# A fused attention and MoE kernel: a fourth unit of work with v in float32, a third buffer for q and M, and one ordering edge on ScalarE

## The chip, the core and the metric

The kernel runs on one core of a Trainium2 chip. The metric is device time in microseconds (us), the median of three runs; smaller is better. The engines are TensorE (PE in the profile, with PEld for its weight loads), VectorE (DVE), ScalarE (ACT), GpSimd (POOL) and SyncE (SP), which here only issues DMAs. Each engine works through its own list of instructions in order, and semaphores tie the lists together.

## What is computed

Two steps follow each other. The first is attention with a memory, for 4 batches, 8 heads, 576 tokens and 64 columns a head. The second is a feed-forward block on its result, 2304 tokens of 512 columns, with a hidden width of 2048:

```python
scores = (q @ k.T) / sqrt(D), causal;  a = softmax(scores);  local = a @ v
q_p = phi(q)                           # max(q, 0) + min(exp(q), 1)
mem_out = (q_p @ M_prev) / (q_p @ z_prev + 1e-6)
x = g * mem_out + (1 - g) * local      # g = sigmoid(beta), one number a head
h = x @ w_in;  r = max(h, 0);  out = (r * r) @ w_out
```

## The kernel before

**Units.** Attention is cut into units: a batch b, a pair p of heads, and a list of query tiles. The list `order` starts with batch 0, tiles [1, 2], pairs 0 to 3 (units one to four, `order[0]` to `order[3]`) and goes on with batch 0, tiles [3, 4], pairs 0 to 3 (units five to eight). The first 64 tokens of each batch are handled ahead of all units by `first_tokens`. `attention` (line 354) handles one unit. It takes exp and phi of q (lines 388 to 402), the memory part `pm` (line 445), and then for each query tile the scores `sp` (line 479), the masked copy `e` with its row bound (line 500), the exponential (line 520), the weights transposed, the product with v into `acc` (lines 572 to 590), and the sum into `memx` (line 600).

**Two ways to v.** The flag `full` is true for the first `NEF` units with tiles [1, 2]. With it the weights `e` stay float32: PE transposes them into `pxa` (line 535), ScalarE copies these to `aF` (line 540), and PE multiplies `aF` by v in float32 (line 579). Without it v and the weights are split into a high and a low float16 part (lines 410 to 433, 558 and 560), a DMA on SP's queue transposes the weights (line 564), PE multiplies float16 parts (lines 585 to 590), and VectorE adds up the two parts (line 592). The first `NES` = 6 units take their scores from float32 q and k as they are; later ones split them first (lines 369 to 379).

**Loads.** `loads` (line 341) issues the DMAs of a unit: `kd` (k, one buffer), `qm` (M and q, `QB` buffers) and `vv` (v, `VVB` = 2 buffers). A unit calls it for the next unit before its own scores. A load waits until the buffer that it takes has been read for the last time.

**Feed-forward blocks.** Tokens go through `moe` (line 723) in blocks of 256: eight rounds j of an up product (lines 747 to 749, 24 matmuls), Relu and square on ScalarE (lines 753 and 754), a high and a low part (`gh`, `gl`), and a down product (lines 737 to 739, 12 matmuls), which stands one round behind. Block 0 is the first 64 tokens of all batches. In its round j = 6 it also prepares block 1: `prefetch` (line 625) reads three quarters of block 1's tokens back from the DRAM tensor `xd`, into which units one to three were written (line 611), transposes them into `px` (line 635), transposes the last quarter straight from unit four's `memx` (line 637, `tail`), and makes `xh` and `xl` (lines 640 and 641). `px` and `up` share two PSUM buffers (tag "up"), so the up product of block 0's last round needs a `px` that has been read.

**What sets the order.** Each engine's list is set when the kernel is built, by a scheduler that plays the program against a model of the chip. A change of a few instructions moves many others. `later` (line 148) adds an edge that only orders: the instruction x stands on its engine behind the one kept in `gate`. `ORD` (line 82) builds units two to four together with block 0, and the rest of the units behind them.

Of the kernel before, what the change touches and what calls it, by code (L numbers as in the profile page):

```python
# [8 lines left out]
F32 = mybir.dt.float32  # L9
# [6 lines left out]
ALU = mybir.AluOpType  # L16
# [22 lines left out]
GHN = 4  # L39
GLV = range(7)  # L40
VMIN = 2.0**-80
NEF = 3
NES = 6
PXT = 'av'
PXE = 'aa'
PHI = 1
QB = 2
VVB = 2
ZW = D + 1
MW = 576  # L50
# [42 lines left out]
def fused_kernel(ctx: ExitStack, tc: tile.TileContext, t0_d, kk_d, qv_d, beta, w_in, w_out, out):  # L93
    nc = tc.nc
# [17 lines left out]
        out=mask, in_=mask, pattern=[[-1, MW]], compare_op=ALU.is_ge, fill=-1e30, base=448, channel_multiplier=1  # L112
# [33 lines left out]
    gate = {}  # L146

    def later(eng, x):
        if eng in gate:
            tc.add_manual_dep(x.ins, gate[eng].ins.name, AFTER, reason="first tokens lead")  # L150
        return x
# [189 lines left out]
    def loads(b, p, tiles):  # L341
        qa, qb = QT[tiles[0]][0], sum(QT[tiles[-1]])
        kd = at.tile([P, S], F32, tag="kd", name="kd", bufs=KB)
        nc.sync.dma_start(kd[:, :qb], kk_d[b, p, :, :qb])
        qm = at.tile([P, 2 * ZW + SQ], F32, tag="qm", name="qm", bufs=QB)
        qa, qb = qa - D + 2 * ZW, qb - D + 2 * ZW
# [7 lines left out]
    def attention(b, p, tiles, ld, after, early, sfull, full):  # L354
# [13 lines left out]
        if not sfull:  # L368
# [4 lines left out]
                out=ql[:, qa:qb], in0=q_raw[:, qa:qb], in1=qh[:, qa:qb].bitcast(F32), op=ALU.subtract  # L373
# [11 lines left out]
        pe = at.tile([P, 2, S], F32, tag="e", name="pe", bufs=EB)[:, 0]  # L385
        w = slice(qa, qb)
        lead = (b, p, tiles) == order[0]
        ex = nc.scalar.activation(pe[:, w], q_raw[:, w], AF.Exp)
        if lead:
            later("s2", ex)  # L390
        ph = pe if sfull else q_raw
        if PHI and not sfull:
            nc.scalar.activation(q_raw[:, w], q_raw[:, w], AF.Relu)
            nc.vector.scalar_tensor_tensor(
                out=q_raw[:, w], in0=pe[:, w], scalar=1.0, in1=q_raw[:, w], op0=ALU.min, op1=ALU.add
            )
        else:
# [3 lines left out]
                out=ph[:, w], in0=q_raw[:, w], scalar=0.0, in1=pe[:, w], op0=ALU.max, op1=ALU.add  # L401
# [3 lines left out]
        if not full:  # L405
# [11 lines left out]
                out=vy, in0=vy, scalar1=VMIN, scalar2=2.0**-VEXP, op0=ALU.max, op1=ALU.mult  # L417
# [6 lines left out]
            if VL[late] == "d":  # L424
                nc.scalar.activation(vh, vr, AF.Copy, scale=vy)
                for h in range(2):
                    nc.vector.scalar_tensor_tensor(
                        out=vl[:, h], in0=vr[:, h], scalar=vy, in1=vh[:, h], op0=ALU.mult, op1=ALU.subtract
# [8 lines left out]
        for grp in (tiles[:2], tiles[2:]):  # L437
# [4 lines left out]
            for j, i in enumerate(grp):  # L442
# [8 lines left out]
                out=nm[:, :ng], in0=pv[:, :, :, D], scalar=1e-6,  # L451
                in1=gi[:, None, h0 : h0 + 2].to_broadcast([P, ng, 2]), op0=ALU.add, op1=ALU.mult,
# [4 lines left out]
                out=memx[:, i0 - 1 : i0 - 1 + ng].rearrange("p i (h d) -> p i h d", h=2),  # L457
                in0=pv[:, :, :, :D],
                in1=nm[:, :ng, :, None].to_broadcast([P, ng, 2, D]),
                op=ALU.mult,  # L460
# [50 lines left out]
        for i in [t for t in TORD if t in tiles]:  # L511
# [6 lines left out]
            for h in range(2):  # L518
                bs = mx[:n, h, ns - 1 : ns]
                ex = nc.scalar.activation(  # L520
                    e[:n, h, :ke], e[:n, h, :ke], AF.Exp, bias=bs, scale=-1.0, accum_out=sm[:n, h : h + 1]
                )
            behind[:] = [ex]
            u0, ur = e[:n, :, 0:D], e[:n, :, D:ke]
            if full:
# [3 lines left out]
                for b0 in range(0, 2 * nb, 4):  # L529
                    bn = min(4, 2 * nb - b0)  # L530
                    px = ps.tile([P, 4, P], F32, tag=PXT, name="pxa", bufs=2)
                    for x in range(bn):
                        h, c = divmod(b0 + x, nb)
# [9 lines left out]
            else:  # L543
# [15 lines left out]
                for x, o0, w in ((ur, P, i * P), (u0, 0, D)):  # L559
                    nc.vector.scalar_tensor_tensor(  # L560
                        out=av[:, :, o0 + w : o0 + 2 * w], in0=x, scalar=SC, in1=av[:, :, o0 : o0 + w],
# [4 lines left out]
                out=sm[:n], in0=sm[:n], scalar=1e-9, in1=gm[:n, h0 : h0 + 2] if full else vz[:n],  # L566
# [6 lines left out]
            if full:  # L573
                s3 = acc[:, :, 0]
# [7 lines left out]
            else:  # L582
# [8 lines left out]
                s3 = at.tile([P, 2, D], F32, tag="s3", name="s3", bufs=1)  # L591
# [6 lines left out]
            for h in range(2 if FX[late] != "p" or full else 0):  # L598
                xo = memx[:n, i - 1, h * D : (h + 1) * D]
                nc.vector.scalar_tensor_tensor(  # L600
                    out=xo, in0=s3[:n, h], scalar=sm[:n, h : h + 1], in1=xo,
# [23 lines left out]
    def prefetch(b, blk, tail=None):  # L625
        nk = NK if tail is None else NK - 1
        xh = mo.tile([P, NK, BLK], F32R, tag="xh", name="xh", bufs=2)
        xl = mo.tile([P, NK, BLK], F32R, tag="xl", name="xl", bufs=2)
        for t in range(2):
            r0 = QT[1 + 2 * blk + t][0]  # L630
            src = mo.tile([P, DM], F32R, tag="x", name="xn", bufs=XB)
            nc.sync.dma_start(src.bitcast(F32)[:, : nk * P], xd[b][r0 : r0 + P, : nk * P])
            px = ps.tile([P, NK, P], F32R, tag="up", name="px", bufs=2)
            for k in range(nk):
                nc.tensor.transpose(px[:, k], src[:, k * P : (k + 1) * P], identr)
            if tail is not None:
                nc.tensor.transpose(px.bitcast(F32)[:, nk], tail[:, t], ident)
            px = px.bitcast(F32)
            ts = slice(t * P, (t + 1) * P)
            nc.scalar.copy(xh[:, :, ts], px)  # L640
            nc.vector.tensor_tensor(out=xl[:, :, ts], in0=px, in1=xh[:, :, ts].bitcast(F32), op=ALU.subtract)
        return xh, xl

    def pair_tiles():
# [78 lines left out]
    def moe(n):  # L723
# [17 lines left out]
        for j in range(NF // 2):  # L741
# [20 lines left out]
            if n == NBLK - 3 and j in (3, PJ):  # L762
                if j == 3:
                    xq.append(pair_tiles())
                pair_prefetch(xq[-1], int(j == PJ))
                yield
            elif j == PJ and n + 1 < NBLK:
                assert n > 0 or last
                xq.append(prefetch(*blocks[n + 1], *last))
                last.clear()  # L770
                yield
# [48 lines left out]
    order = []  # L820
# [8 lines left out]
    def attn(i0, i1):  # L829
        for i in range(i0, i1):  # L830
            ld = nxt.pop()

            def after():
                if i + 1 < len(order):
                    nxt.append(loads(*order[i + 1]))

            yield from attention(*order[i], ld, after, i < NEARLY, i < NES, i < NEF and max(order[i][2]) < 4)

# [60 lines left out]
```

## Time and profile before

| what | value |
|---|---|
| time, median of 3 runs | 578.53 us (578.21 to 580.98) |
| the profiled execution | 578.71 us, span from first to last instruction 576.9 us |
| PE busy | 550.8 us (95% of the span) |
| DVE, ACT, POOL busy | 414.0, 349.6, 63.7 us |
| granted TensorE clock, mean | 0.994 of full speed |

In the page's strip of 40 slices PE stands at nine tenths or more from 10% of the span on, with one weaker slice (8 at a quarter of the way, near 100 us), where the granted clock falls to 7 tenths. Matmuls are pipelined, so the time that a matmul costs is read from one start to the next, not from its own duration. In the profile's rows an instruction on float32 operands at lines 479, 445 and 579 shows as two rows. The rows themselves stand further down, in numbered groups.

### The profile page before, as it was taken

How to read it: one execution, taken by the hardware profiler on the slowest of the kernel's cores; microseconds unless marked ns; L12 is line 12 of the kernel's file. 1: busy time of each engine (PE TensorE's matmuls, PEld its weight loads, DVE VectorE, ACT ScalarE, POOL GpSimd, SP SyncE). 2: the span in 40 equal slices, each digit the busy share in tenths (PEclk: the TensorE clock that was granted, in tenths of full speed). 3: DMA queues.
4: the chain of work that ended last, by engine and by line, in shares of the span. 5: the costliest groups of instructions: out<-in, count | busy, mean ns of one | idle time of the engine just before them, and what ended most of it. 6: DMA issues, size and time to landing. Idle time of an engine off the chain costs nothing.

```text
span 576.9 us, 11597 instructions
## 1 busy us (share of the span) xinstructions
PE 550.8 (95%) x4259; PEld 478.6 (83%) x4259; DVE 414.0 (72%) x1323; ACT 349.6 (61%) x792; POOL 63.7 (11%) x45
## 2 busy tenths in 40 slices
PE   5489998898999999999999999999999999999997
PEld 5378886787888888898988988889889898888885
DVE  6989989897989888989695988969787523212121
ACT  4589976767868767877567675665756222212213
POOL 3749560012010000000000000000000000000000
PEclk9999999799999999999999999999999999999999
DMA  8857654875665466676456736675244610000001
GB/s 310 341 192 286 228 168 111 174 162 136 138 150 159 109 183 151 149 185 168 110 108 124 149 78 163 115 189 143 56 84 83 128 37 1 36 2 0 1 0 73
DMA packets 124856, 74.71 MB, mean 129 GB/s; under 512 B 97152, under 2 KB 110464, under 8 KB 124800
## 3 DMA queue, kind: packets, MB, share of 16 engines
q1 hardware_dynamic: 124800, 73.98, 49.7%
q8 instruction: 33, 0.54, 0.4%
q14 instruction: 23, 0.19, 0.1%
HBM read 41.59 MB, written 8.78 MB: 87 GB/s over the span
## 4 chain that ended last, share of the span: by engine, by line
PE 63%; DVE 12%; ACT 10%; DMA 9%; issue 3%; POOL 1%; SPq 1%; ACTq 0%; DVEq 0%; POOLq 0%
PE oacc L677 8%; PE up L747 6%; PE up L749 6%; PE up L748 6%; PE oacc L737 6%; PE oacc L739 6%; PE oacc L738 6%; PE sp L479 5%; DMA vv<-in_qv_dram 4%; ACT e L520 3%; PE up L692 3%; PE up L691 3%; PE up L693 3%; PE acc L590 2%; PE pm L445 2%
## 5 line engine op out<-in xcount | busy, mean ns | idle before, releaser
L747 PE MATMUL up<-xh,w 128*128 128x256 f32 x448 | 129.5, 289 | 0.0
L748 PE MATMUL up<-xl,w 128*128 128x256 f32 x448 | 128.9, 288 | 0.0
L749 PE MATMUL up<-xh,w 128*128 128x256 f32 x448 | 128.4, 287 | 0.0
L520 ACT ACTIVATE e<-e,mx 128x320 f32<-128x320 f32 (+3 forms) x128 | 77.6, 608 | 50.1 <-DVE memx L600 34.1
L737 PE MATMUL oacc<-w,gh 128*128 128x512 f32 x224 | 89.9, 402 | 0.0
L747 PEld LDWEIGHTS up<-xh,w 128*128 128x128 f32 x448 | 86.0, 192 | 2.9 <-issue 0.6
L738 PE MATMUL oacc<-w,gh 128*128 128x512 f32 x224 | 88.4, 395 | 0.0
L748 PEld LDWEIGHTS up<-xl,w 128*128 128x128 f32 x448 | 86.1, 192 | 2.2
L739 PE MATMUL oacc<-w,gl 128*128 128x512 f32 x224 | 86.4, 397 | 0.4 <-DVE gl L759 0.4
L749 PEld LDWEIGHTS up<-xh,w 128*128 128x128 f32 x448 | 86.1, 192 | 0.7
L560 DVE SCALAR_TENSOR_TENSOR a<-e,a 128x128 f16<-128x128 f32 x116 | 64.1, 566 | 31.1 <-ACT a L558 30.1
L558 ACT ACTIVATE a<-e 128x128 f16<-128x128 f32 x116 | 55.0, 524 | 10.9 <-DMA aT<-a 9.9
L753 ACT ACTIVATE r<-up 128x512 f32<-128x512 f32 x56 | 32.7, 584 | 43.2 <-PE up L749 29.0
L702 DVE CAST gh<-r 128x512 fp32r<-128x512 f32 x15 | 6.4, 427 | 62.4 <-ACT r L701 62.4
L739 PEld LDWEIGHTS oacc<-w,gl 128*128 128x128 f32 x224 | 41.5, 188 | 9.0 <-DVE gl L759 0.9
L738 PEld LDWEIGHTS oacc<-w,gh 128*128 128x128 f32 x224 | 42.3, 189 | 6.6
L500 DVE CUSTOM_DVE_ANT_0 e<-sp,mask 128x320 f32<-128x320 f32 (+3 forms) x128 | 47.0, 417 | 0.9 <-PE sp L479 0.7
L737 PEld LDWEIGHTS oacc<-w,gh 128*128 128x128 f32 x224 | 42.3, 189 | 6.4
L700 ACT ACTIVATE r<-up 128x512 f32<-128x512 f32 x16 | 9.6, 597 | 60.8 <-PE up L693 60.8
L759 DVE TENSOR_TENSOR gl<-r,gh 128x512 fp32r<-128x512 f32 x56 | 38.9, 695 | 2.6 <-ACT gh L756 1.8
L677 PE MATMUL oacc<-w,gh 128*128 128x512 f32 x120 | 36.8, 389 | 0.0
L590 PE MATMUL acc<-vs,aT 128*128 128x128 f16 x302 | 36.7, 220 | 0.0
(153 smaller groups left out, 1160.2 us busy)
## 6 DMA issues: line engine op xcount, KB each, us to landing
raw<-in_w_in_dram SPq DMA_DIRECT2D x11, 512.0 KB, 7.2
vv<-in_qv_dram SPq DMA_DIRECT2D x16, 320.0 KB, 3.3
raw<-in_w_out_dram SPq DMA_DIRECT2D x9, 512.0 KB, 6.6
kd<-in_kk_dram SPq DMA_DIRECT2D x16, 288.0 KB, 3.1
out_dram<-o SPq DMA_DIRECT2D x16, 256.0 KB, 2.1
xd<-memx SPq DMA_DIRECT2D x31, 128.0 KB, 1.9
xn<-xd SPq DMA_DIRECT2D x14, 256.0 KB, 2.9
qm<-in_qv_dram SPq DMA_DIRECT2D x8, 321.0 KB, 2.9
```

Of the source, the lines that this page charges most:

```text
L500: nc.vector.tensor_tensor_reduce(out=e[:, h, ka:kb], in0=sps[:, h, cs], in1=mask[:, 448 - q0 + ka : 448 - q0 + kb], scale=-0.125, scalar=3 ...
L520: ex = nc.scalar.activation(e[:n, h, :ke], e[:n, h, :ke], AF.Exp, bias=bs, scale=-1.0, accum_out=sm[:n, h : h + 1])
L558: nc.scalar.mul(av[:, :, o0 : o0 + w], x, SC)
L560: nc.vector.scalar_tensor_tensor(out=av[:, :, o0 + w : o0 + 2 * w], in0=x, scalar=SC, in1=av[:, :, o0 : o0 + w], op0=ALU.mult, op1=ALU.sub ...
L590: nc.tensor.matmul(o2, aT[:, h * nb + c, :n], vs[:, h, c], start=False, stop=c == i)
L677: mms.append(nc.tensor.matmul(acc[t], g[:, ts], w_out_op(f, part), start=s0, stop=s1))
L737: nc.tensor.matmul(acc[t], gh[:, u, ts], w_out_op(f, 0), start=f == 0, stop=False)
L738: nc.tensor.matmul(acc[t], gh[:, u, ts], w_out_op(f, 1), start=False, stop=False)
L739: nc.tensor.matmul(acc[t], gl[:, u, ts], w_out_op(f, 0), start=False, stop=f == NF - 1)
L747: nc.tensor.matmul(up[:, u, :], w_in_op(f, k, 0), xh[:, k, :], start=k == 0, stop=False)
L748: nc.tensor.matmul(up[:, u, :], w_in_op(f, k, 0), xl[:, k, :], start=False, stop=False)
L749: nc.tensor.matmul(up[:, u, :], w_in_op(f, k, 1), xh[:, k, :], start=False, stop=k == NK - 1)
```

## The change

Three things change. `NEF` goes from 3 to 4, so unit four (batch 0, pair 3, tiles [1, 2]) takes the float32 way to v. `QB` goes from 2 to 3, so `qm` has three buffers. And the exponential of q of the sixth unit (`order[5]`) gets an ordering edge on ScalarE: it stands behind the last copy to `xh` of block 1's `prefetch` (the key "v3" is set and not used).

```diff
-NEF = 3
+NEF = 4
...
-QB = 2
+QB = 3
...
         lead = (b, p, tiles) == order[0]
+        second = (b, p, tiles) == order[5]
         ex = nc.scalar.activation(pe[:, w], q_raw[:, w], AF.Exp)
         if lead:
             later("s2", ex)
+        if second:
+            later("s3", ex)
...
-            nc.scalar.copy(xh[:, :, ts], px)
-            nc.vector.tensor_tensor(out=xl[:, :, ts], in0=px, in1=xh[:, :, ts].bitcast(F32), op=ALU.subtract)
+            c = nc.scalar.copy(xh[:, :, ts], px)
+            d = nc.vector.tensor_tensor(out=xl[:, :, ts], in0=px, in1=xh[:, :, ts].bitcast(F32), op=ALU.subtract)
+            if tail is not None:
+                gate["s3"], gate["v3"] = c, d
```

In the counts of instructions, PE loses unit four's 16 float16 matmuls and one small one (`vt`), and gains 10 transposes at line 535 and 10 float32 matmuls at line 579. ScalarE gains 8 copies (line 540) and loses 5 instructions. VectorE loses 14. SP loses two transposing DMAs. In the changed kernel, lines from 389 to 643 carry numbers up to 3 higher, and those behind it 5 higher.

The first place is PE's list where block 1 is prepared. The names ending in 924 and 902 are unit four's `memx` before and after, `acc_1028` is unit four's product before, `acc_956` and `acc_1018` are its products after (tile 2, tile 1), `sp_1552` before is unit six's scores, `sp_1464` after is unit five's second group, and `up_1335` is block 0's last up product. Before:

```order
L587 MATMUL acc_1028<-vs_913,aT_957 128x64
L590 LDWEIGHTS aT_957
L590 MATMUL acc_1028<-vs_913,aT_957 128x128
L414 LDWEIGHTS vx_1403
L414 MATMUL vt_1408<-identb_74,vx_1403 128x128
L635 MATMUL px_1307<-identr_67,xn_1305 128x128 x3
L635 MATMUL px_1316<-identr_67,xn_1314 128x128 x3
L637 MATMUL px_1316<-identr_67,memx_924 128x128
L445 MATMUL pm_1419<-qm_934,pe_1399 128x130 x2
L479 MATMUL sp_1552<-kd_1426,qm_1428 128x448 x2
L479 MATMUL sp_1552<-kd_1426,qm_1428 128x64 x2
L747 MATMUL up_1335<-xh_116,w24_1091 128x256
```

After, with 24 rows of block 0's last up product behind the last row, then unit six's first scores:

```order
L638 MATMUL px_1293<-identr_67,xn_1291 128x128 x3
L638 MATMUL px_1302<-identr_67,xn_1300 128x128 x3
L582 MATMUL acc_956<-vv_775,aF_941 128x64 x6
L538 MATMUL pxa_1000<-identr_67,e_934 64x128
L538 MATMUL pxa_1000<-identr_67,e_934 128x128
L538 MATMUL pxa_1000<-identr_67,e_934 64x128
L538 MATMUL pxa_1000<-identr_67,e_934 128x128
L640 MATMUL px_1302<-identr_67,memx_902 128x128
L482 MATMUL sp_1464<-kd_917,qm_919 128x512 x2
L582 MATMUL acc_1018<-vv_775,aF_999 128x64 x4
L417 LDWEIGHTS vx_1389
L417 MATMUL vt_1394<-identb_74,vx_1389 128x128
```

Unit four's two products with v now stand behind the first rows on `px`, where they stood ahead of them, and the last up product of block 0 stands ahead of unit six's first scores, where it stood behind them.

The second place is SP's queue at the same time. `memx_763` is unit three's result; `qm_1428` before and `qm_1414` after are unit six's q and M, `qm_1547` and `qm_1533` unit seven's; `vv_1431` and `vv_1417` are unit six's v, `vv_937` and `vv_922` unit five's; `kd_1426` and `kd_1412` are unit six's k. Before:

```order
L351 DMA vv_937<-in_qv_dram 128x640
L564 DMA_TRANSPOSE aT_957<-a_956 128x10x128
L611 DMA xd0_91<-memx_763 128x2x128
L564 DMA_TRANSPOSE aT_957<-a_956 128x6x128
L632 DMA xn_1305<-xd0_91 128x384
L632 DMA xn_1314<-xd0_91 128x384
L348 DMA qm_1428<-in_qv_dram 128x130
L348 DMA qm_1428<-in_qv_dram 128x256
L351 DMA vv_1431<-in_qv_dram 128x640
L344 DMA kd_1426<-in_kk_dram 128x576
```

After:

```order
L351 DMA vv_922<-in_qv_dram 128x640
L348 DMA qm_1533<-in_qv_dram 128x130
L614 DMA xd0_91<-memx_763 128x2x128
L348 DMA qm_1533<-in_qv_dram 128x256
L635 DMA xn_1291<-xd0_91 128x384
L635 DMA xn_1300<-xd0_91 128x384
L344 DMA kd_1412<-in_kk_dram 128x576
L351 DMA vv_1417<-in_qv_dram 128x640
L567 DMA_TRANSPOSE aT_1437<-a_1436 128x14x128
```

Unit four's two transposing DMAs are gone, unit six's `qm` has moved to a place ahead of these rows and unit seven's stands here instead, around the write of unit three's result; unit six's v has moved behind its k.

The third place is ScalarE's list there. `e_1438` before and `e_1424` after are unit five's tile 3, `pe_1518` and `pe_1504` the sixth unit's exponential of q, `qh_1623` a copy of unit seven's q, `aF_941` and `aF_999` unit four's transposed weights. Before:

```order
L756 CAST gh_1297<-r_1296 128x512
L520 ACTIVATE e_1438,sm_1440<-e_1438,mx_1439 128x448 x2
L425 ACTIVATE vs_913<-vv_775,vy_903 128x2x3x64
L558 ACTIVATE a_1450<-e_1438 128x2x64
L558 ACTIVATE a_1450<-e_1438 128x2x384
L388 ACTIVATE pe_1518<-qm_1428 128x256
L640 CAST xh_1303<-px_1316 128x4x128
```

After:

```order
L389 ACTIVATE pe_1385<-qm_919 128x256
L371 CAST qh_1623<-qm_1533 128x256
L543 COPY aF_941<-pxa_942 64x128 x2
L543 COPY aF_941<-pxa_942 128x256
L543 COPY aF_941<-pxa_950 128x256
L523 ACTIVATE e_1424,sm_1426<-e_1424,mx_1425 128x448 x2
L561 ACTIVATE a_1436<-e_1424 128x2x64
L561 ACTIVATE a_1436<-e_1424 128x2x384
L543 COPY aF_999<-pxa_1000 64x128 x2
L543 COPY aF_999<-pxa_1000 128x128 x2
L643 CAST xh_1289<-px_1302 128x4x128
L389 ACTIVATE pe_1504<-qm_1414 128x256
```

The sixth unit's exponential of q has gone behind the first copy to `xh` (as the edge asks), and the copy of unit seven's q has come to stand ahead of unit four's copies.

## Rows read from the trace of the kernel before

**Rows 1.** Busy time by stretch: us, each engine, granted clock, DMA share, GB/s
```profile
87.06:95.50 8.44, 8.44 (x46) 6.80 (x45) 7.38 (x26) 6.80 (x23) 0.92 (x2) 1.00 0.27 62
95.50:102.20 6.70, 3.98 (x34) 2.41 (x33) 6.48 (x26) 1.62 (x4) 0.00 (x0) 1.00 0.84 222
102.20:109.10 6.90, 5.88 (x26) 4.74 (x25) 5.91 (x23) 4.69 (x10) 0.84 (x1) 0.51 0.71 162
112.10:220.00 107.90, 105.41 (x860) 91.64 (x862) 93.23 (x329) 81.45 (x193) 7.50 (x6) 1.00 0.62 151
220.00:570.00 350.00, 350.00 (x2530) 305.37 (x2527) 222.44 (x727) 184.03 (x404) 0.00 (x0) 1.00 0.40 91
```

**Rows 2.** Waits of PE from 86 to 112.1 us: total, times, longest
```profile
PE pm L445 <- DVE s L592: 1.2, 1, 1.2
PE acc L585 <- DVE vs L427: 1.1, 1, 1.1
PE sp L479 <- DMA kd<-in_kk_dram: 1.0, 1, 1.0
PE px L635 <- DMA xn<-xd: 0.3, 1, 0.3
```

**Rows 3.** Timeline of PE, two stretches: start us, us, what, xcount
```profile
81.15 1.38 PE L579 MATMUL acc<-vv,aF 64*128 64x64 f32 x8
82.46 0.50 PE L738 MATMUL oacc<-w,gh 128*128 128x512 f32 x1
...
84.44 0.55 PE L579 MATMUL acc<-vv,aF 128*128 128x64 f32 x4
84.83 0.60 PE L535 MATMUL pxa<-identr,e 128*64 128x128 f32 x4
85.18 0.36 PE L747 MATMUL up<-xh,w 128*128 128x256 f32 x1
```

**Rows 4.** Timeline of PE from 86.9 to 112.1 us, some rows
```profile
86.94 0.28 PE L749 MATMUL up<-xh,w 128*128 128x256 f32 x1
87.06 0.40 PE L737 MATMUL oacc<-w,gh 128*128 128x512 f32 x1
...
89.90 0.32 PE L579 MATMUL acc<-vv,aF 64*128 64x64 f32 x1
...
92.23 0.22 PE L414 MATMUL vt<-identb,vx 128*128 128x128 bf16 x1
...
95.26 0.61 PE L445 MATMUL pm<-qm,pe 128*128 128x130 f32 x4
...
97.72 1.13 PE L479 MATMUL sp<-kd,qm 64*128 64x512 f32 x4
...
98.78 0.23 PE L585 MATMUL acc<-vs,aT 128*128 128x128 f16 x1
...
99.07 0.22 PE L414 MATMUL vt<-identb,vx 128*128 128x128 bf16 x1
...
99.62 0.90 PE L635 MATMUL px<-identr,xn 128*128 128x128 f32 x6 [0.33 <-DMA xn<-xd]
...
103.86 2.18 PE L479 MATMUL sp<-kd,qm 64*128 64x448 f32 x8 [1.02 <-DMA kd<-in_kk_dram]
...
112.08 0.38 PE L747 MATMUL up<-xh,w 128*128 128x256 f32 x1
```

**Rows 5.** Timeline of SP's DMA issues
```profile
94.91 0.52 SPq L611 DMA_DIRECT2D xd<-memx  x1
...
99.53 0.38 SPq L344 DMA_DIRECT2D kd<-in_kk_dram  x1
```

**Rows 6.** DMAs of line 351 (v) over the whole run
```profile
DMA to landing us min/median/max: 2.4/3.3/7.9
```

**Rows 7.** Timeline of VectorE
```profile
109.16 1.01 DVE L427 SCALAR_TENSOR_TENSOR vs<-vv,vy,vs 128x320 f16<-128x320 f32 x2
```

**Rows 8.** Timeline of ScalarE at the sixth unit's exponential of q
```profile
101.99 0.42 ACT L388 ACTIVATE pe<-qm 128x256 f32<-128x256 f32 x1 [2.81 <-DMA qm<-in_qv_dram]
```

## The prediction, made before the changed kernel ran

> **What bounds the kernel now.** I read the busy times by stretch first. From 220 us to 570 us PE is busy for 350.00 of 350.00 us at full clock, and from 112.1 to 220 us for 105.41 of 107.90 [rows 1]. In these 458 us a microsecond comes back only if PE has less to do, or if one of the last 2.5 us of idle time goes. [...]
>
> **The change part by part.** The sum is made against the profiled execution, 578.71 us, which is 0.18 us above the median.
>
> *Work of PE.* Unit four's float32 product with v takes, for tile 2, from 81.15 to 82.46 and from 84.44 to 84.83 us in unit three, 1.70 us; for tile 1, two of the first kind less (1.31 + 0.39 / 2 - 0.15, about 1.36). Four transposes take 84.83 to 85.18, 0.35 us, so ten take 0.9 [rows 3]. That is +4.0 us. What goes are 16 float16 matmuls: six of them take from 98.78 to 99.07, 0.29 us [rows 4], so 16 take 0.8, and 0.1 for the small one. Net **+3.1 us**, all on PE's path, since PE is the bound behind this place.
>
> *Waits and clock.* I walk down PE's list of the changed kernel from 87.06 us, up to which both lists hold the same work apart from its order, with durations of rows. The first two down matmuls, unit five's first scores and the rest of unit three take 0.5 + 2.33 (89.90 to 92.23) + 0.4 for `pm`; from 92.23 to 95.26 stand 12 down matmuls and the small one, so 0.24 each [rows 4]. Twenty down matmuls, which stood in part ahead of this before, now come here: 87.1 + 3.2 + 0.5 (waits for `gh`) + 4.6 = 95.4. Six transposes and two down matmuls end at 96.4. Now PE needs the tokens read back for block 1. From the issue of the write of unit three's result to PE's first row on them took 99.62 - 94.91 = 4.71 us [rows 4, 5]. The write can be issued some 2.4 us earlier than before, near 92.5, since two transposing DMAs are gone and VectorE has no float16 split to do: 97.2, a **wait of 0.8**. Then 0.7 for `px`, 1.7 for tile 2's product, 0.35 for four transposes: 100.0. The next rows wait for VectorE to write `memx` and to empty unit five's first scores, about **0.6**: 100.6. Scores as before 97.72 to 98.78, 1.06: 101.7. Tile 1's product 1.4: 103.1. Block 0's last up product, 24 times 0.12 (86.94 to 87.06): 106.0 [rows 4]. Unit six's k may be issued when the scores have ended, at 101.7; before, it took 103.86 - 99.53 = 4.3 us until PE went on [rows 4, 5]: 106.0, so it just fits. Scores 1.2 (2.18 at half the clock before [rows 4]), one transpose and `pm` 0.5: 107.7.
>
> What PE wants then is unit five's v in two parts, and this is where the change gives time back. Unit four now reads `vv` until its last matmul at 103.1, so unit six's v can be issued only then (before, the float16 split freed the buffer much earlier), and with the median landing of 3.3 us [rows 6] VectorE's next step on it, which stands ahead of unit five's split in VectorE's list, starts near 106.4. Behind it I estimate 0.7 for this step and 1.4 for the low part of unit five's weights with some small ones, by the 1.0 that the split on as many columns takes [rows 7]; then the split itself, 1.0: 109.4, a **wait of 1.7**. Seven float16 matmuls later PE wants block 1's second half of tokens, and in VectorE's list unit six's row bounds and `xl` itself stand ahead, six larger steps that I put at 2.1 us together: 111.9, a **wait of 2.0**. So block 1 starts at 111.9 where it started at 112.08 [rows 4], with four scores of 1.06 us still to do that were done before. The stretch comes out at -0.2 + 1.06 = **+0.9 us**: 6.6 us of old waits and slow clock go, 3.1 us of work and about 4.5 us of new waits come. The bounds: with v's landing at its least, 2.4 us, 0.9 earlier; if the tokens or v land 1.5 us later, +2.4.
>
> *The third `qm` buffer.* Before, ScalarE sat 2.8 us before the sixth unit's exponential of q, waiting for `qm`, with block 1's `xh` copy behind it [rows 8]. With the third buffer that load moves some rows up on SP's queue, and the edge puts the exponential behind the copy, so this wait can hold up nothing of block 1. But the copy of unit seven's q now stands ahead of unit four's `aF` copies on ScalarE, and its load stands on SP behind the write of unit three's result (92.5). ScalarE therefore stands still from about 91.7 to 96. PE does not notice: it has 20 down matmuls until 95.4 and wants `aF` only at 97.9, and the copies take 1 us. With a landing 1.5 us later this cover is gone, and each further 1 us costs PE 1 us. The edge itself costs nothing, since GpSimd and VectorE need that exponential only behind `xl`.
>
> *Later waits.* The 2.5 us from 112.1 to 220 [rows 1] come from VectorE, which is busy for 93.23 of 107.90 us there. `qm` comes earlier for all later units (for: fewer waits), and unit six stands about 1 us later (against). I leave them at 2.5, with bounds of 0.5 and 4.5.
>
> Sum: 578.71 + 0.9 = **579.6 us**, 0.2% above the median of 578.53. A measurement of this kernel tells about 0.5% (2.9 us) from no change, so this is no change.
>
> **The rivals.** *The two waits at 108 to 112 us don't come* (faster). They hang on one landing and on VectorE's list. If unit six's v lands before VectorE asks, or VectorE is some 2 us ahead because unit four's float16 split (about 3 us of its work) is gone, both shrink: -3.7, and with the earlier `qm` -1.5 of the later waits: 574.4. For it: VectorE had only 0.2 us of idle time from 95.5 to 102.2 [rows 1], so work taken off it there counts. Against: in the changed list it waits itself, for v and for PE.
>
> *The clock falls again* (slower). In my walk PE does 0.4 us of work between 107.7 and 111.9. In the kernel before, 3.98 us of work in 6.70 us were followed by the half clock for 6.8 us [rows 1]. If PE idles for 2.7 us or more there, the fall may come behind it instead of ahead, while block 1 runs: +2.9 us (half of 5.88, as before), 582.5. The deciding point is whether the two waits together exceed about 2.7 us. What the row shows ahead of the old fall is a stretch in which the last matmuls were transposes [rows 4]. [...]
>
> *It does not do what it says.* Block 1 may hang on unit three's tokens, written and read back through memory, and not on unit four; then only the work counts, +3.1 less the clock's 2.9: 578.9, inside no change.
>
> **How the numbers follow.** The walk 0.34 and the last rival 0.04 make no change 0.38, with their own range of 576 to 581.4; the faster rival 0.30; the fall of the clock 0.32. The range leaves out the ends beyond the faster rival with 1 us more, 573.5, and beyond the clock's with the later waits' upper bound of 2, 584.0 (rounded down).
>
> **What would show it.** Right: PE's waits on the split of v (line 430 there) and on `xl` between 107 and 113 us, over 1 us each; no wait of PE on unit six's k; 10 more transposes and 10 more float32 products for 4 us. The faster rival: PE busy for over 9.5 us of each 10 from 95 to 115 us and no half clock. The slower one: a half clock that starts after 105 us. Wrong altogether: a wait of PE on `aF` near 97 us of over 1 us, or idle time of PE behind 220 us.

## The result: 1.1% slower, and the profile of the changed kernel

The changed kernel takes 586.67 us (median of 6 runs, 583.88 to 587.59), the kernel before 578.86 us in the same comparison. The ratio on record is 1.011, with a 95% interval from 1.0083 to 1.0138 (the two medians alone would give 1.0135). The ratios here and below leave out three executions in the slow state, all of pq_qb2 and pq_qb3. The prediction was 579.6 us and "no change", and its range ended at 584.0: the measured loss is clear of no change, and the time lies 2.7 us above the range. The profiled execution took 586.79 us with a span of 585.0 us, 8.1 more than the span before. Line numbers of the changed kernel are up to 5 higher than those of the kernel before.

Busy time of the engines by stretch, the same five stretches as in [rows 1], with the same columns:

```profile
87.06:95.50 8.44, 8.22 (x47) 6.37 (x46) 6.36 (x22) 5.00 (x16) 1.69 (x2) 1.00 0.30 79
95.50:102.20 6.70, 6.33 (x40) 4.41 (x38) 3.66 (x14) 5.17 (x17) 0.00 (x0) 1.00 0.17 59
102.20:109.10 6.90, 6.15 (x48) 5.18 (x45) 5.22 (x15) 5.93 (x12) 0.84 (x1) 1.00 0.70 159
112.10:220.00 107.90, 101.64 (x841) 87.43 (x841) 91.76 (x328) 79.33 (x191) 6.34 (x6) 1.00 0.68 154
220.00:570.00 350.00, 348.13 (x2506) 304.26 (x2505) 219.49 (x726) 183.25 (x401) 0.00 (x0) 1.00 0.40 91
```

The place that the change works on came out well: from 95.5 to 109.1 us PE is busy for 12.48 of 13.60 us at full clock, where it was busy for 9.86 us, 5.88 of them at half clock. The loss stands in the last two lines. Behind 112.1 us PE idles for 107.90 - 101.64 = 6.26 us where it idled for 2.49, and behind 220 us for 1.87 where it idled for nothing.

The timeline of PE and of VectorE (DVE) from 97 to 112 us (start, duration, what), to lay beside the walk of the prediction and [rows 4, 7]:

```profile
97.29 0.91 PE L638 MATMUL px<-identr,xn 128*128 128x128 f32 x6
...
101.16 1.13 PE L482 MATMUL sp<-kd,qm 64*128 64x512 f32 x4 [0.15 <-DVE mx L503]
...
106.45 1.19 PE L482 MATMUL sp<-kd,qm 64*128 64x448 f32 x8
...
107.73 0.61 PE L448 MATMUL pm<-qm,pe 128*128 128x130 f32 x4
110.21 0.23 PE L588 MATMUL acc<-vs,aT 128*128 128x128 f16 x1 [1.86 <-DMA aT<-a]
...
110.50 0.36 PE L752 MATMUL up<-xh,w 128*128 128x256 f32 x1
```

```profile
107.12 0.82 DVE L413 TENSOR_REDUCE vx<-vv 128x1 f32<-128x640 f32 x1 [1.55 <-DMA vv<-in_qv_dram]
...
109.32 1.01 DVE L430 SCALAR_TENSOR_TENSOR vs<-vv,vy,vs 128x320 f16<-128x320 f32 x2
...
111.81 0.69 DVE L644 TENSOR_TENSOR xl<-px,xh 128x512 fp32r<-128x512 f32 x1
```

PE's waits behind that place (what waits, released by what, us in total, times, longest), from 112 to 182 us and then from 182 to 310 us:

```profile
PE vt L417 <- DVE s L595: 1.9, 2, 1.2
PE sp L482 <- DVE mx L503: 1.0, 2, 0.7
PE sp L482 <- DVE vx L415: 0.9, 1, 0.9
PE acc L588 <- DMA aT<-a: 0.8, 2, 0.5
...
```

```profile
PE acc L588 <- DMA aT<-a: 1.8, 1, 1.8
```

The loss from 112 to 182 us is not one wait but eleven small ones on many things (6.4 us in all); the one near 300 us is for a transposing DMA, and the granted clock falls behind it. The windows from 299.5 to 307 us show both:

```profile
299.50:303.50 4.00, 2.24 (x26) 1.91 (x24) 1.26 (x5) 1.55 (x7) 0.00 (x0) 1.00 0.49 116
303.60:307.00 3.40, 3.40 (x35) 3.40 (x34) 2.83 (x14) 1.60 (x6) 0.00 (x0) 0.50 0.43 81
```

At the granted clock of 0.50 I put the 3.40 us of work at 1.7 us more than at full clock, half of it; the rows of the up product stand 0.21 us apart there (from 306.03 to 306.45 us), where they stood 0.12 apart at full clock (from 299.24 to 299.96 us). So of the 8.1 us some 3.8 are new idle time up to 220 us, 1.9 idle time behind it, 1.7 this clock; the prediction left the waits up to 220 us unchanged, and its sum had nothing for the idle time and the clock behind them. The question for the experiments is which of the three parts of the change brings them, and by what.

### The profile page after: what moved, and what is told of

It reads as the page before. It is cut to its first block, busy times and chain, and to the rows that moved or that the text cites. A ratio compares the mean times of both kernels' runs of the same rounds, so it can differ in the third digit from the quotient of the medians.

```text
span 585.0 us, 11595 instructions
## 1 busy us (share of the span) xinstructions
PE 553.7 (95%) x4272; PEld 480.7 (82%) x4272; DVE 406.7 (70%) x1309; ACT 349.8 (60%) x795; POOL 62.0 (11%) x45
## 4 chain that ended last, share of the span: by engine, by line
PE 49%; DVE 19%; DMA 14%; ACT 10%; issue 4%; POOL 2%; SPq 1%; ACTq 0%; DVEq 0%; POOLq 0%
PE oacc L682 7%; DMA vv<-in_qv_dram 5%; PE oacc L742 4%; PE oacc L743 4%; PE oacc L744 4%; PE up L752 4%; PE up L754 4%; PE up L753 4%; ACT e L523 4%; DVE e L503 3%; PE sp L482 3%; DVE a L563 3%; DMA aT<-a 3%; PE up L698 2%; PE up L697 2%
## 5 line engine op out<-in xcount | busy, mean ns | idle before, releaser
L563 DVE SCALAR_TENSOR_TENSOR a<-e,a 128x128 f16<-128x128 f32 x112 | 62.4, 571 | 25.3 <-ACT a L561 24.9
L561 ACT ACTIVATE a<-e 128x128 f16<-128x128 f32 x112 | 53.1, 529 | 12.9 <-DMA aT<-a 12.3
```

The costliest lines, as they stand in the source:

```text
L561: nc.scalar.mul(av[:, :, o0 : o0 + w], x, SC)
L563: nc.vector.scalar_tensor_tensor(out=av[:, :, o0 + w : o0 + 2 * w], in0=x, scalar=SC, in1=av[:, :, o0 : o0 + w], op0=ALU.mult, op1=ALU.sub ...
```

## The experiments

The medians of "before" differ by up to 1.8 us between comparisons, so ratios to before are what is compared. Three theories stood at the start: **A**, unit four's late release of v; **B**, the third buffer, whose loads stand elsewhere on SyncE's queue; **C**, the redrawn order as such. A fourth, **E**, came later.

### The parts alone and in pairs

```diff
nef4:       -NEF = 3   +NEF = 4        (kernel before)
qb3:        -QB = 2    +QB = 3         (kernel before)
edge:       only the lines with "second" and "s3" (kernel before)
nef4_qb3:   without "if second: later("s3", ex)" (changed kernel)
nef4_edge:  -QB = 3    +QB = 2         (changed kernel)
qb3_edge:   -NEF = 4   +NEF = 3        (changed kernel)
```

> The kernel before with the fourth unit in float32 alone (two q buffers, no edge). Theory A, the late v (unit four reads v until its last matmul, so unit six's v comes some 3 us later, and the attention of the next units runs late through blocks 1 and 2): the whole loss is here, 584 to 588 us, with over 4 us of TensorE idle time more than before from 112 to 182 us. Theory B, the third q buffer (its loads stand ahead of the transposing DMAs and token writes on SyncE's queue): 577 to 581 us, since only the 3.1 us of work come and the 6.6 us of old losses may go. Theory C, the redrawn order (each variant gets another order of the attention in blocks 1 to 3, and with it other waits): 575 to 585, with the waits of 112 to 182 us at other places than in the changed kernel.

> The kernel before with the third buffer for q and M alone. Theory A (late v): no loss, 577 to 580 us, the half clock of 102 to 109 us stays. Theory B (third q buffer): 582 to 586 us, with SyncE's transposing DMAs of aT behind q loads, and TensorE waiting for aT from 112 to 182 us. Theory C (redrawn order): 576 to 583 us, the sign open.

> The kernel before with the edge alone (the sixth unit's exponential of q behind block 1's copies). Theory A and theory B: 578 to 580 us, nothing changes behind 112 us, for the exponential is needed only behind that copy. Theory C (redrawn order): up to 4 us either way, since the edge alone already redraws TensorE's list.

> The changed kernel without its edge. Theories A and B: as the changed kernel, 585 to 588 us. Theory C (redrawn order): anything from 578 to 588 us; over 3 us away from the changed kernel speaks for it, for the edge itself holds up an exponential that nobody waits for.

> The changed kernel with two q buffers again (fourth unit in float32 and the edge). So far: fourth unit alone 579.75 us, third buffer alone 582.92, edge alone 581.61, fourth unit and third buffer 585.61, the changed kernel 586.67. Theory B (the third q buffer is what costs, once the fourth unit stands with it): 578 to 581 us. Theory C (redrawn order, the parts do not add up): 576 to 586; if the parts did add, the fourth unit's 0 and the edge's +2.6 would give 582. Theory A (late v): 584 to 588.

> The changed kernel with the fourth unit not in float32 (third q buffer and edge). Theory B: 582 to 584 us, the third buffer's loss without anything from the edge. Sum of the parts: 582.9 + 2.6 = 585.5. Theory C: neither, 577 to 587 with the waits at other places than with the third buffer alone (which has no TensorE wait from 112 to 182 us and waits of 3.4 us for aT behind 182).

Measured, as ratio to before with its 95% interval:

| | two buffers | three buffers |
|---|---|---|
| neither | 1 | 1.0044 (1.0021 to 1.0066) |
| fourth unit | 0.9999 (0.9972 to 1.0026) | 1.0109 (1.0081 to 1.0138) |
| edge | 1.0047 (1.0026 to 1.0068) | 1.0154 (1.0129 to 1.0178) |
| fourth unit and edge | 0.9981 (0.9963 to 0.9999) | 1.0110 (1.0083 to 1.0138), the change |

Every row loses by the third buffer, by 0.4 to 1.3%. The second row and the last are the same two programs, each measured twice: beside the fourth unit the edge changes no instruction and no wait on any engine, so nef4_edge is nef4, and the changed kernel is nef4_qb3. The two measurements of each agree within 0.2%, and the fourth unit is no loss by either. Theory A falls. B has the right part. C has its share too, since the parts do not add up: the edge alone costs 0.5%, with the third buffer 1.1% more than that buffer alone, and beside the fourth unit nothing, because there it does nothing. qb3_edge (589.13 us) came out slower than any theory had it, edge (581.61 us) above the 578 to 580 us of A and B, and qb3 has none of the waits for `aT` from 112 to 182 us that B forecast.

### More buffers of another kind

The fourth unit with a third buffer for v, or with a second one for k, each with two buffers for q.

```diff
nef4_vvb3:  -VVB = 2   +VVB = 3
nef4_kb2:   -KB = 1    +KB = 2
```

> The fourth unit in float32 and a third buffer for v in place of the one for q. Theory A' (what the later waits hang on is v: VectorE waits for it 9.2 us from 100 to 182 us in the changed kernel, 5.2 before, 6.4 with the fourth unit alone): VectorE's wait for v falls under 3 us, the wait of TensorE for the split of v near 108 us goes, and the time is 574 to 577 us. Theory C (redrawn order): 577 to 584 us whatever VectorE's wait for v is.

> The fourth unit in float32 and a second buffer for k. With one k buffer SyncE stood before the load of k for TensorE's scores for 8.9 us (2 times) from 90 to 182 us with the fourth unit alone, with the loads of v and the transposing DMAs behind it. Theory D (it is SyncE's standing before loads whose buffer is taken that makes the later loads late): VectorE's wait for v falls under 4 us and the time is 575 to 578. Theory C: 577 to 584, no relation.

Measured: 582.95 us, ratio 1.0054 (1.0032 to 1.0075), and 581.78 us, 1.0032 (1.0010 to 1.0053). With the third v buffer VectorE's wait for v from 100 to 182 us went from 6.4 to 1.0 us, as theory A' had it, and with the second k buffer to 3.5 us, as theory D had it; the time went up all the same. Waits of nef4_vvb3 from 100 to 182 us (VectorE) and from 112 to 182 us (PE):

```profile
DVE gl L759 <- ACT gh L756: 2.7, 1, 2.7
DVE qm L394 <- ACT qm L393: 2.4, 3, 0.9
...
DVE vx L410 <- DMA vv<-in_qv_dram: 1.0, 1, 1.0
```

```profile
PE sp L479 <- DVE mx L500: 2.6, 2, 1.4
PE sp L479 <- DVE ql L372: 2.0, 2, 1.1
```

The waits moved to other things. A' and D fall.

### Which units, and which queue

In q3_early and q3_late the third buffer has a name of its own and serves units three, six and nine, or twelve and fifteen; the other units take turns in two. In pq_qb3 and pq_qb2 the loads of q and M are issued by GpSimd, with three and two buffers (the rest is the changed kernel).

```diff
q3_early, q3_late:
-        qm = at.tile([P, 2 * ZW + SQ], F32, tag="qm", name="qm", bufs=QB)
+        n = order.index((b, p, tiles))
+        tag, bufs = ("q3", 1) if n in THIRD else ("qm", 2)   # (2, 5, 8) or (11, 14)
+        qm = at.tile([P, 2 * ZW + SQ], F32, tag=tag, name="qm", bufs=bufs)
pq_qb3, pq_qb2:
-            nc.sync.dma_start(qm[:, c0:c1], qv_d[b, p, :, c0:c1])
+            nc.gpsimd.dma_start(qm[:, c0:c1], qv_d[b, p, :, c0:c1])
```

> The changed kernel with the third buffer for q and M in use for the first eleven of the sixteen units only (the loads until about 152 us); the later ones take turns in two. Two q buffers with the other two parts gave 579.29 us, three 586.67. If the third buffer's price lies in the waits of 112 to 182 us (3.9 us more idle time of TensorE there than with two buffers): 582 to 584, without the gap and the half clock near 300 us. If it lies only in the place near 300 us (1.8 us of waiting for aT and 1.7 us of half clock): 579 to 580.5. Theory C (redrawn order): any value from 576 to 588.

> The changed kernel with the third buffer in use from the twelfth unit on only (two places, units twelve and fifteen). If the two prices stand each for itself: up to 182 us as with two buffers (2.3 us idle from 112 to 182), and a wait for aT with a half clock near 300 us, 582 to 583.5. If the waits of 112 to 182 us are what brings the later ones: 579 to 580. Theory C: any value from 576 to 588.

> The changed kernel (three q buffers) with the loads of q and M issued on GpSimd's queue, away from SyncE's. Theory B' (the price comes from loads of q that stand on SyncE's queue ahead of the transposing DMAs of aT and the loads of v): within 2 us of its partner with two buffers (pq_qb2), and the landing of aT from 182 to 310 us falls from a median of 4.7 us to under 4.0. Theory C (the redrawn order of TensorE and VectorE): its distance to the partner stays at 5 us or more.

> Its partner: two q buffers, the fourth unit in float32, the edge, and the loads of q and M on GpSimd's queue. Theory B': 577 to 581 us, as on SyncE's queue (579.29), and as its partner. Theory C: 576 to 586, since this too redraws the order.

Measured: q3_early 1.0109 (1.0077 to 1.0141), q3_late 1.0035 (1.0018 to 1.0053), pq_qb3 1.0283 (1.0242 to 1.0323), pq_qb2 1.0083 (1.0054 to 1.0112). Taken by themselves, these numbers say that the early use carries the whole price. q3_early lies above both forecasts of the two prices, and the wait for `aT` that was forecast for q3_late did not come. Taking q's loads off SyncE's queue did not take the third buffer's price away: the two kernels lie 2.0% apart, and both are slower than their partners with q on SyncE's queue. B' falls.

What led on was that q3_early and nef4_edge have the same list on PE from about 177 us on, and yet q3_early went on losing. At one place, near 350 us, with the same rows around it and the load of v issued 4.0 us ahead in both, the transposing DMA of `aT` held SyncE's queue for 3.1 us in q3_early and 1.8 in nef4_edge. Counted over all runs, 13 or 14 of the 42 or 43 transposing DMAs behind 182 us take over 2.4 us in qb3, nef4_qb3, qb3_edge, the changed kernel and q3_early, 16 of 46 in pq_qb3, and 0 to 5 in before, nef4, edge, nef4_edge, nef4_vvb3, nef4_kb2, pq_qb2 and q3_late. (nef4 has 4 and nef4_edge, the same program, none: so few are scatter.) The order does not part these groups. Where the tiles lie does. In SBUF (the memory on the chip) the tiles stand one behind the other. A buffer of q and M is 642 x 4 = 2568 bytes, and the next one starts 2592 bytes behind it (the two of the kernel before at 9152 and 11744). So a third one, allocated ahead of the two tiles `a`, the sources of the transposing DMAs, moves the larger one (18 blocks of 128 x 128) from byte 45056 (a multiple of 512) to 47648 (32 bytes past one), and the smaller one (6, 10 and 14 blocks) from 40448 to 43040, 32 bytes past one as well. In q3_late the third buffer is allocated behind both, and they stay where they were. This is **theory E**.

### The offset, with every list unchanged

Four kernels change only the width of a buffer. The instructions and waits of all engines stand in the same order as in the kernel each is made from (for after_64 the changed kernel, for the other three nef4_edge).

```diff
after_64:   -qm = at.tile([P, 2 * ZW + SQ], ...   +qm = at.tile([P, 656], ...
ne_32:      -kd = at.tile([P, S], ...             +kd = at.tile([P, S + 8], ...
src32:      -a = at.tile([P, tg * P], ...         +a = at.tile([P, tg * P + 16], ...
dst32:      -a = at.tile([P, tg * P], ...         +a = at.tile([P, tg * P + 16 * (tg == 18)], ...
            -aT = at.tile([P, tg, P], ...         +aT = at.tile([P, tg * P + 16 * (tg == 18)], ...
```

> The changed kernel, every engine's list word for word the same, with the buffers of q and M 656 columns wide in place of 642, so that the three take a multiple of 64 bytes and the tiles behind them in SBUF, the weights a and aT of the transposing DMAs among them, start on multiples of 64 bytes again (in the changed kernel they start 32 bytes off one). Theory E (the third buffer's price is this offset: it makes the wider transposing DMAs hold SyncE's queue some 0.8 us longer, 1.9 to 2.7 us): 577.5 to 580.5 us, the transposing DMAs behind 182 us under 2.4 us but for a few (13 of 42 were over it), TensorE's idle time from 112 to 182 us about 2.5 us. Theory C (the redrawn order): 585.5 to 587.5 us, unchanged, since the order is the same.

> The other way round: two q buffers, the fourth unit in float32 and the edge (579.29 us), every list the same, with k's buffer 32 bytes wider, so that all tiles behind it start 32 bytes off a multiple of 64. Theory E: 584 to 588 us, 12 or more of the 42 transposing DMAs behind 182 us over 2.4 us (none was). Theory C: 578.5 to 580.

> The same with only the wider a (their source) 32 bytes off. Theory E with the source as the cause: 583 to 588 us. With the destination as the cause: 578.5 to 580. Theory C: 578.5 to 580.

> Two q buffers, the fourth unit in float32 and the edge, lists the same, with only the wider aT (the destination of the transposing DMAs of 18 and 14 blocks) 32 bytes off a multiple of 64. Theory E with the destination as the cause: 583 to 588 us. With the source (a) as the cause: 578.5 to 580. Theory C: 578.5 to 580.

| | source `a` starts past a multiple of 512 bytes by | DMAs over 2.4 us behind 182 us | us | ratio to before |
|---|---|---|---|---|
| nef4_edge | 0 | 0 of 42 | 579.29 | 0.9981 (0.9963 to 0.9999) |
| dst32 (destination moved by 32) | 0 | 1 of 42 | 581.19 | 1.0014 (0.9987 to 1.0041) |
| src32 | 32 | 13 of 42 | 585.64 | 1.0101 (1.0066 to 1.0137) |
| ne_32 | 32 | 15 of 43 | 585.12 | 1.0083 (1.0051 to 1.0115) |
| after_64 | 128 | 13 of 43 | 584.08 | 1.0084 (1.0057 to 1.0110) |

Moving the source by 32 bytes, with nothing else changed in what is done or in which order, makes the program 1.2% slower (1.0% against its other measurement, nef4). In src32 the tiles allocated behind the larger `a` move too, by 64 bytes. In dst32 they move by the same 64 bytes (its `aT` by 32), while the source stays; against dst32 src32 is 0.9% slower. ne_32, where every tile behind k's buffer moves by 32 bytes, loses no more than src32. The destination does not show in the DMAs: the 0.3% of dst32, above its forecast of 578.5 to 580 us, lies within overlapping intervals. The transposing DMAs of nef4_edge from 200 to 260 us and of src32 from 203 to 264 us, the same ten in both (line, queue, count: shortest/median/longest ns on SyncE's queue, first and last start; then from issue to landing):

```profile
L567 SPq DMA_TRANSPOSE aT<-a x10: 1273/1924/2260, 205.6 to 259.2; - x10
...
DMA to landing us min/median/max: 2.6/3.9/4.8
```

```profile
L567 SPq DMA_TRANSPOSE aT<-a x10: 1272/2229/3140, 208.6 to 263.1; - x10
DMA to landing us min/median/max: 3.0/4.6/5.0
```

It is the widest of them that became longer. Behind 182 us there are 12 with 18 blocks of 128 x 128: their median is 1.92 us in nef4_edge and 2.70 in src32, and all 12 are over 2.4 us there. The 12 with 14 blocks have 1.47 and 1.48, and those with 10 and 6 blocks stay at 1.33 and 1.23; but their source, the smaller `a`, has not moved in src32. In ne_32 it has: the 14-block ones hold the queue for 1.53 us, those with 10 and 6 blocks for 1.35, so the queue feels it little. They do land later. From issue to landing those with 10 blocks take 3.53 us in ne_32 against 3.06 in nef4_edge and 3.05 in src32, those with 6 blocks 2.87 against 2.55 and 2.60 (medians). after_64 missed its forecast of 577.5 to 580.5: its sources were on multiples of 64 bytes, and 13 DMAs were still long. That corrects the theory rather than ending it. In the runs with few long DMAs the sources stand on multiples of 512, in nef4_kb2 (4 of 43, median of the 18-block ones 1.85 us) at 256 past one; 32 and 128 past one are long (medians of 2.7 us). What sets these two pairs of offsets apart, and why, no run shows.

### The changed kernel with its sources back in place

```diff
after_512, qb3_edge_512:
-        qm = at.tile([P, 2 * ZW + SQ], F32, tag="qm", name="qm", bufs=QB)
+        qm = at.tile([P, 688], F32, tag="qm", name="qm", bufs=QB)
```

> The changed kernel, every list word for word the same, with the buffers of q and M 688 columns wide, so that the sources a of the transposing DMAs start on multiples of 512 bytes in SBUF, as in the kernel before. With 656 columns they started 128 bytes off, and 13 of 43 transposing DMAs behind 182 us still took over 2.4 us; in all runs with few such DMAs the sources start on multiples of 256 or 512 bytes, in all with many they are 32 or 128 off. Theory E' (the source's offset from a multiple of 256 bytes is what costs): at most 5 such DMAs, TensorE's idle time from 112 to 182 us under 4 us, no wait of 1.8 us or more for aT near 300 us, 578.5 to 581.5 us. Theory C (redrawn order): 585 to 587.5 us.

> The kernel with the third buffer and the edge and without the fourth float32 unit (589.13 us, the slowest with q's loads on SyncE), every list the same, sources on multiples of 512 bytes. Theory E': 579 to 583 us and at most 5 transposing DMAs over 2.4 us behind 182 us. Theory C: 588 to 590.

Measured: after_512 takes 580.43 us, ratio 0.9996 (0.9979 to 1.0012), where the changed kernel, with the same lists, has 1.0110. No transposing DMA behind 182 us is over 2.4 us. So the offset of the tiles behind the buffer is the price of the change: 1.1%, some 6.6 us; that it is the source's among them rests on src32 and dst32. qb3_edge_512 takes 584.87 us, 1.0063 (1.0041 to 1.0085), against 1.0154, with 1 of 42 DMAs over 2.4 us: here 0.9% are the offset, and 0.6% stay. That is outside both forecasts, 579 to 583 and 588 to 590 us. Busy time from 112 to 182 and from 182 to 310 us in after_512, the changed kernel and src32, in this order:

```profile
112.00:182.00 70.00, 67.78 (x572) 58.69 (x571) 63.57 (x230) 54.73 (x136) 6.36 (x6) 1.00 0.65 157
182.00:310.00 128.00, 127.27 (x1053) 111.65 (x1052) 112.90 (x398) 97.69 (x219) 0.00 (x0) 1.00 0.64 152
```

```profile
112.00:182.00 70.00, 63.74 (x540) 54.59 (x540) 58.44 (x213) 50.93 (x126) 6.34 (x6) 1.00 0.68 151
182.00:310.00 128.00, 126.13 (x1028) 110.31 (x1027) 110.22 (x386) 94.04 (x213) 0.00 (x0) 0.99 0.67 151
```

```profile
112.00:182.00 70.00, 65.97 (x544) 56.19 (x544) 58.91 (x212) 51.28 (x126) 7.70 (x6) 1.00 0.65 153
182.00:310.00 128.00, 126.46 (x1029) 111.31 (x1028) 108.09 (x376) 92.42 (x210) 0.00 (x0) 1.00 0.60 145
```

With the source in place PE idles for 2.22 us from 112 to 182 us, with it 32 bytes off for 6.26 us in the same lists (src32, in the other order: 4.03, where nef4_edge has 2.34). And the DMAs themselves, ten from 200 us on in the changed kernel, then the same ten in after_512:

```profile
L567 SPq DMA_TRANSPOSE aT<-a x10: 1247/2419/2950, 206.0 to 257.3; - x10
...
DMA to landing us min/median/max: 2.8/4.7/6.3
```

```profile
L567 SPq DMA_TRANSPOSE aT<-a x10: 1232/1840/2369, 200.1 to 251.1; - x10
...
DMA to landing us min/median/max: 2.6/3.9/5.4
```

The 18-block ones behind 182 us have a median of 2.69 us in the changed kernel and 1.84 in after_512 (12 each), and in these windows the median landing is 0.8 us later. SyncE issues its DMAs in the order of its list, so the loads of k, q and v and the writes of `memx` behind a longer one can start later too: in the changed kernel an 18-block one held the queue from 248.36 to 251.09 us, and the write of `memx` behind it was issued at 251.14. That fits PE's waits in the changed kernel, which are small ones on many things. Whether the longer hold of the queue or the later landing brings the loss, no run shows.

What stays open: the rest of 0.6% in qb3_edge_512, the 0.3 to 0.5% of edge, q3_late, nef4_vvb3 and nef4_kb2, and the 0.8% of pq_qb2, all with the 18-block source on a multiple of 256. I put them down to the redrawn order, but no run shows it. The third buffer alone with its source in place was not run. With the offset it costs 0.4%, though 14 of its 42 DMAs are long, and PE has no wait from 112 to 182 us, only behind that. Either the price of the offset hangs on the order around it or the third buffer gives something back there; no run parts the two. Its window from 112 to 182 us:

```profile
112.00:182.00 70.00, 70.00 (x592) 60.76 (x589) 63.74 (x228) 55.42 (x139) 7.28 (x6) 1.00 0.67 155
```

## Why the prediction was wrong, step by step

**Work of PE, +3.1 us: right.** PE is busy for 551.2 us in after_512, at full clock, and was busy for 550.8 us with 2.9 us of half clock in it: +3.3 us. In the changed kernel it is 553.7, less 1.7 for the half clock near 305 us: +4.1.

**The walk to block 1: right to a microsecond, and 1.4 us too slow at its end.** First rows on the tokens read back at 97.29 us (97.2 in the walk), unit six's scores at 106.45 (106.0), `pm` done at 110.21 - 1.86 = 108.35 (107.7), the split of unit five's v started at 109.32 and done about a microsecond later (done at 109.4 in the walk). The wait of 0.8 for the tokens did not show, since PE came to them later by itself. The first of the two late waits came, 1.86 us for 1.7; the row names the DMA of `aT`, which landed 6.1 us after its issue at 104.0, that is at 110.1, and the first half of the split had ended 0.3 us earlier: without the DMA the wait would have been only that much shorter. The wait of 2.0 for `xl` did not come: `xl` started at 111.81, where the walk had it done at 111.9, but block 1's first matmul reads only `xh` and could start at 110.50. Two of the walk's numbers do not add up, without changing its end: 20 down products at 0.24 are 4.8 us, not 4.6, and its new waits (0.8, 0.6, 1.7, 2.0) are 5.1 us, not about 4.5. The 6.6 us of old waits and slow clock are read from [rows 1]: 2.72 and 1.02 us in which PE stood idle, and 2.9 us as half of the 5.88 us of work at a granted clock of 0.51. The changed kernel has 1.12 us of idle time in those 13.60 us, at full clock.

**The half clock of 102 to 109 us: gone in this profile**, as in those of nef4_edge, after_512 and src32. It is not settled by the list, though. ne_32 has the lists of nef4_edge, and from 100.5 to 107.2 us it stood at half clock (first line), where nef4_edge did not (second line):

```profile
100.50:107.20 6.70, 6.54 (x25) 5.15 (x25) 4.53 (x15) 4.82 (x12) 0.84 (x1) 0.50 0.32 90
100.50:107.20 6.70, 6.70 (x48) 5.45 (x49) 4.73 (x14) 5.59 (x13) 0.85 (x1) 1.00 0.65 138
```

So the ten new transposes, which stand in both lists, do not decide it either way. The rival of the clock named the right kind of loss at the wrong place: 1.7 us from 303.6 us on, and behind 1.76 us of idle time where that rival asked for 2.7.

**The third buffer, costed at nothing: this is the step that failed.** I followed the loads, the queue and ScalarE's stall, and all that was harmless: after_512, with the same lists, takes 0.9996 of the time before. I did not ask what else a buffer does: it takes room, and moves every tile allocated behind it. That moved the sources of the transposing DMAs 32 bytes off, the 18-block ones held SyncE's queue for 2.69 us instead of 1.84, and the kernel lost 1.1%. The trace of before had the durations of the transposing DMAs, but nothing in it says that they hang on an address. The edge, which the prediction credits with keeping the exponential off block 1's `xh` copy, did nothing: with the fourth unit in float32 the lists hold that order without it.

**Later waits, 2.5 us with bounds of 0.5 and 4.5: mis-sized for the same reason.** Measured from 112.1 to 220 us: 6.26 us. With the source in place (after_512) it is 2.22 us in the same stretch, inside the bounds. The bounds came from rows of before alone, and so took for granted that each DMA would take as long as before. And "idle time of PE behind 220 us", which the prediction named as what would show it wrong altogether, came.

Without the offset the forecast would have stood: 0.9996 for the same lists (0.9979 to 1.0012), against 1.0019 predicted, both no change. It is no close test of the walk, whose 1.4 us too many are 0.2% of the time.

## What to carry to other kernels

A change in the number or size of a buffer changes addresses: after it, look at where the sources of transposing DMAs start, and pad so that they stand on multiples of 512 bytes (256 by the one run that had it); here the 18-block ones went back from 2.69 to 1.84 us by it. When waits appear in many places at once, compare the durations of the same DMA rows in both traces before blaming the order; two kernels with the same lists and one moved tile are the cleanest test there is. And give a buffer's cost a term of its own, for the room that it takes.

## What the runs showed of the hardware

- A transposing DMA of 18 blocks of 128 x 128 in float16 whose source starts 32 or 128 bytes past a multiple of 512 holds its queue for 2.7 us where it holds it for 1.8 to 2.1 with the source on the multiple (medians of 12 in each run). One of 14 blocks takes 1.5 to 1.8 us either way. An offset of 32 bytes in the destination did nothing to it (1.93 us). With every list unchanged, sources off their place cost 0.8 to 1.2% of this kernel; why 18 blocks hold the queue longer and 14 do not, no run shows.
- The smaller ones with their source off hold the queue hardly longer, but land later: 10 blocks after 3.5 to 3.8 us instead of 3.0 to 3.3, 6 blocks after 2.9 to 3.0 instead of 2.5 to 2.7 (medians of each run, behind 182 us).
- A wait of PE in dense work can be followed by a slower clock. In the changed kernel, behind 1.76 us for `aT` at 300 us the granted clock was at 0.50 for 3.4 us. But behind 2.0 us for `px` in nef4_vvb3 it did not fall (granted clock 1.00 from 300 to 570 us, where that wait stands). The same program shows falls in one execution and none in another: nef4 and nef4_edge are the same on every engine, and their profiled executions have a mean granted clock of 0.982 and 1.000.
